# The last pair's products of h ordered by bank, one q load behind the late chunks, the rest of the values added a step later

## The chip, the cores and the metric

One Trainium2 chip, one of its cores. The metric is the device time of one execution in microseconds (us).

## The reference

Attention with pooled keys and values, and a gated layer behind it:

```python
k_p = k.reshape(B, H, Sp, 8, D).mean(axis=3)      # B=8, H=8, S=576, D=64, Sp=72
v_p = v.reshape(B, H, Sp, 8, D).mean(axis=3)
scores = scale * np.matmul(q, k_p.transpose(0, 1, 3, 2))
attn = softmax(scores)                             # with 1e-09 in the divisor
x = (attn @ v_p).transpose(0, 2, 1, 3).reshape(4608, 512)
h = x @ w_in                                       # 512 x 2048
g = h * np.clip(h + 3.0, 0.0, 6.0) / 6.0
out = g @ w_out                                    # 2048 x 512
```

All in float32; the kernel splits operands into a high and a low part and adds three matmuls for each product.

## The kernel before

The 4608 tokens are twelve blocks. The first four ("plain", `run`) go through the 16 slices f of the hidden size one by one: a product of h on PE (L847, into bank h0 or h1 by turns), relu on ACT (L855), the gate on DVE (L859), the high part on ACT (L863), the low part on DVE (L867), and two slices later the product with w_out (L878).

The last eight blocks go in four pairs, the super blocks n = 0 to 3 (`super_block`). Two slices of the hidden size, two halves of the input and the two blocks are each taken as a 2 x 2 matrix of blocks, and its product is made with seven products instead of eight. For each pair i of slices there are seven kinds o of products of h (L1140). Kinds 1, 6, 7 and 4 go into the pair's bank X, 5 and 3 into Y, 2 into Z. What comes behind a product: after 1, 5 and 6 ACT copies the bank (`keep`, L1113); after 2, 3 and 7 DVE adds bank and copy (`plus`, L1104) and the gate follows, relu on ACT (L1096) and the gate itself on DVE (L1098); after 4 the gate comes at once. A product into a bank whose reader is still due waits for it. The order of the products is the list `N1`, made from the table `PERIOD`, whose entries are a kind and by how many pairs it lags. Then comes the second half of the super block, the products with w_out (L1194 in n = 0, L1267 in the others, where g is split by L1119 on ACT and L1121 on DVE).

The weights of the seven products are made by `sums_of` during plain blocks 2 and 3 (DVE, tile wq), stored to DRAM (L954) and loaded again in each super block as chunks of two products, in the order of `N1`, 512 KB each (`chunk`, L998; wd0 to wd27 are the chunks in DRAM). There are seven places for chunks: four, wsFalse, are there from the middle of block 3, three, wsTrue ("late"), come free at its end. The hook `more` runs at the end of block 3: it takes the two first loads of the next pair's attention ahead, the q load and a load of the rest of the values (tile vr), and then loads the three late chunks.

Between the products stand the steps of the attention of later blocks: loads (q L241, k L249, v L285 and its rest vr L289), sums of eight values (`prep_v`, L384), the rest's high and low parts vrem (L410 on ACT, L411 on DVE), scores on PE (L464, kbd times qt), their maximum on DVE (mx, L468), exponentials on ACT (L473), sum and inverse on DVE (L490, L491), the division on POOL (L502), transposes (L573, L575), splits (alo L586, arem L597 and L599) and the product with the values (L647). `side_steps` gives the order of the loads (`load_v`) and of the additions (`prep_v`) of the values.

The code gives each step a place between products; the scheduler that builds the program then orders each engine's instructions by its own model of when each can run. An engine runs its queue strictly in order, SP's queue of DMAs too, and a DMA also waits until the eighth before it has landed.

Of the kernel before, what the change touches and what calls it, by code (L numbers as in the profile page):

```python
# [22 lines left out]
PLAIN = 4  # L23
# [12 lines left out]


PERIOD = ((1, 0), (2, 0), (7, 1), (5, 0), (6, 0), (4, 1), (3, 0))
RAW = {1: (0, 0), 2: (0, 1), 4: (1, 1)}
CHUNK, NSTREAM, NFIRST, NC, NREL = 2, 7, 4, 3, 2  # L40

# [57 lines left out]
def attention_moe_kernel(  # L99
# [20 lines left out]
    NB, _, NPAIR, S = q.shape  # L120
# [126 lines left out]
    def load_k(b, p):  # L247
        kraw[b, p] = ring("kst")
        nc.sync.dma_start(kraw[b, p], k[b, p])  # L249
        after_mark()  # L250
# [3 lines left out]
    def prep_k(b, p):  # L254

        two = b == 0
        if not two:
            ks = pool.tile([P, 1, SP], F32, name="ksum", bufs=1)
        elif p % 2 == 0:
            ks = ksum[p // 2] = piece(0, 2 * SP).rearrange("p (i s) -> p i s", i=2)  # L260
        else:
            ks = ksum[p // 2]
        i = p % 2 if two else 0
        nc.vector.tensor_reduce(
            out=ks[:, i], in_=kraw.pop((b, p)).rearrange("p (s o) -> p s o", o=POOL), axis=AX.X, op=ALU.add
        )
        after_mark()
        if i == two:

            scale = 1.0 / (POOL * D**0.5)  # L270
            for h in range(2):
                rows = slice(h * D, (h + 1) * D)
                nc.scalar.mul(kbds[b % 2][rows, p - i : p + 1, h * SP : (h + 1) * SP], ks[rows], scale)
# [3 lines left out]
    def load_v(b, p):  # L277

        own = late and b > 2 and p == NPAIR + 1
        t = vraw[b, p] = late[0].tile([P, POOL * D], F32, name="vr") if own else ring("vst")  # L280
        half = slice(p % 2 * (POOL // 2) * D, (p % 2 + 1) * (POOL // 2) * D)
        to = t[:, : POOL * D].rearrange("p (c n) -> p c n", c=2)
        p -= p % 2
        if p < NPAIR:
            nc.sync.dma_start(to, v[b, p : p + 2, :, half].rearrange("c r n -> r c n"))  # L285
            after_mark()
            return
        for c in range(3):
            nc.sync.dma_start(to[c * REM : (c + 1) * REM], vr[b, :, :, half].rearrange("g r n -> r g n"))  # L289
            after_mark()  # L290
# [366 lines left out]
    def side_steps(b):  # L657

        ks = [lambda p=p: load_k(b, p) for p in range(NPAIR)]
        ks += [lambda p=p: prep_k(b, p) for p in range(NPAIR)]  # L660
        if b > 2:
            order = ("load", 5), ("load", 4), ("load", 0), ("load", 1), ("prep", 4), ("load", 2), ("load", 3)
            order += ("prep", 0), None, ("prep", 2)
            do = {"load": load_v, "prep": prep_v}
            return ks, [(lambda x=x: do[x[0]](b, x[1])) if x else no_slot for x in order]
        vs = []
        n = NPAIR + NG
        for p in range(n):
            vs.append(lambda p=p: load_v(b, p))
            if p > 2 and p % 2:  # L670
                vs.append(lambda p=p: prep_v(b, p - 3))
        vs.append(lambda: prep_v(b, n - 2))
        return ks, vs
# [225 lines left out]
    class Paced:  # L899


        def __init__(self, steps, n, more=()):
            self.steps, self.n, self.at, self.done = steps, n, 0, 0
            self.more = list(more)
# [18 lines left out]


    NPR = NF // 2
    N1 = [(i, o) for t in range(NPR + 1) for o, d in PERIOD for i in [t - d] if 0 <= i < NPR]
    supers = range(PLAIN, len(BLOCKS), 2)
    w_dram = [tc.dram_tile([P, CHUNK, 2, 2 * P], F32, name=f"wd{n}") for n in range(len(N1) // CHUNK)]
    w2_dram = [tc.dram_tile([P, 4, 2, 2, DM // 2], F32, name=f"w2d{m}") for m in range(NF // 4)]
    w2t_dram = [tc.dram_tile([P, len(PLACED), 2, 2, DM // 2], F32, name=f"w2t{m}") for m in range(NF // 4)]  # L930

    def dram_of(i, o):
        n = N1.index((i, o))
        return w_dram[n // CHUNK][:, n % CHUNK]

    def pair_of(i):
        return [w_of[2 * i + r, 0].bitcast(F32).rearrange("p m (q c) -> p m q c", q=2) for r in range(2)]
# [18 lines left out]
    def store(to, src):  # L956
        nc.sync.dma_start(to, src)

    def plain_of(i, n):
        if n < 2:  # L960
            for o, (r, q) in list(RAW.items())[2 * n : 2 * n + 2]:
                store(dram_of(i, o), pair_of(i)[r][:, :, q])
# [116 lines left out]
    def super_block(n, j, first_att, second_att):  # L1079
# [4 lines left out]
        r_of, c_of = [], []  # L1084
        paced = Paced(first_att, len(N1) - 2)

# [40 lines left out]

        for m, (i, o) in enumerate(N1):
            if o == 1:
# [287 lines left out]
    later_steps = {}  # L1417
# [83 lines left out]
    def more():  # L1501

        early_x.pop().release()
        more_late.append(tc.alloc_tile_pool(name="late2", bufs=1, side="left", reuse_waits="tile"))
        n_lead = 2
        for pre, *_ in later_steps[PLAIN + 2]:
            while pre and n_lead:
                x = pre.pop(0)
                assert not isinstance(x, tuple) or x[0] == "load"
                (x[1] if isinstance(x, tuple) else x)()  # L1510
                n_lead -= 1
        chunk(0, NSTREAM - 1)

    make = [lambda i=i, h=h: sums_of(i, h) for i in range(NPR) for h in range(2)]
# [71 lines left out]
```

## Time and profile before

| what | value |
|---|---|
| runs | 891.61, 891.85, 892.01 us |
| median | 891.85 us |
| profiled execution, its own time | 891.74 us |
| span of the profile | 890.0 us |
| granted TensorE clock | 0.998 |
| DMA | 200.00 MB, mean 225 GB/s |

PE is the matmul, PEld the load of its weights, which runs ahead of the matmul; a wait stands in brackets behind the row that waited, with what it waited for. The stages lie so: plain blocks 2 and 3 from 217 to 348 us, the h stages of the super blocks at 348 to 426, 496 to 568, 632 to 702 and 767 to 826, and the products with w_out behind each.

### The profile page before, as it was taken

The numbers are of one execution on the slowest core, as the hardware profiler recorded it, in microseconds if no ns is written. First come the engines' busy times: TensorE is split into PE (matmuls) and PEld (weight loads), VectorE is DVE, ScalarE is ACT, GpSimd is POOL, SyncE is SP. The second block draws the span as 40 slices with busy tenths as digits, with TensorE's granted clock in tenths as the row PEclk, the third lists the DMA queues.
The fourth block names the chain that finished last, engine by engine and source line by source line (L and its number), as shares of the span: only waits on it lengthen the run. The fifth ranks groups of instructions, "written<-read, shape, count | busy, mean of one in ns | idle before, by whom it ended". The sixth has DMA issues, their size and how long they took to land.

```text
span 890.0 us, 15637 instructions
## 1 busy us (share of the span) xinstructions
PE 869.6 (98%) x5360; PEld 811.6 (91%) x5360; DVE 667.0 (75%) x1340; ACT 553.0 (62%) x1515; POOL 82.3 (9%) x168
## 2 busy tenths in 40 slices
PE   7899999999999999999999999999999999999998
PEld 7788888988989889999888999899999999999998
DVE  5999864567776785788889588997688877466664
ACT  5998666655666565778444677665576846355442
POOL 4100002110111100102000111100110200000000
PEclk9999999999999999999999999999999999999999
DMA  9980205996435253997596978887986777877884
GB/s 285 393 303 1 72 24 180 356 331 175 120 83 152 56 163 89 360 310 247 191 296 212 359 240 277 270 268 229 300 291 215 238 232 239 277 256 231 273 264 134
DMA packets 124654, 200.00 MB, mean 225 GB/s; under 512 B 13216, under 2 KB 81056, under 8 KB 124576
## 3 DMA queue, kind: packets, MB, share of 16 engines
q1 hardware_dynamic: 124432, 199.00, 68.6%
q8 instruction: 43, 0.70, 0.3%
q14 instruction: 35, 0.29, 0.1%
q10 hardware_dynamic: 144, 0.00, 0.0%
HBM read 158.08 MB, written 40.89 MB: 224 GB/s over the span
## 4 chain that ended last, share of the span: by engine, by line
PE 77%; DVE 9%; DMA 7%; ACT 4%; SPq 2%; issue 1%; DVEq 0%; ACTq 0%
PE psx L1140 23%; PE psx L1267 20%; PE pso L878 10%; PE psh L847 9%; PE psx L1194 8%; PE psa L647 3%; PE psa L464 3%; DMA wd<-wq 2%; DMA stage<-q_l 2%; ACT e L473 2%; SPq L954 1%; DVE wq L950 1%; PE psa L573 1%; DVE wq L945 1%; DMA qt<-q_l 1%
## 5 line engine op out<-in xcount | busy, mean ns | idle before, releaser
L1140 PE MATMUL psx<-x,wsFalse 128*128 128x384 f32 x768 | 150.5, 339 | 3.2 <-DVE g L1104 1.4
L847 PE MATMUL psh<-xhi,w 128*128 128x384 f32 (+2 forms) x520 | 146.2, 340 | 0.1
L1140 PEld LDWEIGHTS psx<-x,wsFalse 128*128 128x128 f32 x768 | 132.8, 188 | 5.0 <-DVE g L1104 1.8
L1119 ACT CAST part<-g 128x768 fp32r<-128x768 f32 x100 | 83.5, 837 | 79.6 <-PE psx L1267 59.5
L1121 DVE TENSOR_TENSOR part<-g,part 128x768 fp32r<-128x768 f32 x100 | 95.3, 954 | 39.5 <-ACT part L1119 39.2
L878 PE MATMUL pso<-w,ghi 128*128 128x512 f32 x384 | 120.7, 399 | 0.4 <-ACT o L883 0.4
L1140 PE MATMUL psx<-x,wsTrue 128*128 128x384 f32 x576 | 116.0, 340 | 0.1
L1267 PE MATMUL psx<-wsFalse,part 128*128 128x256 f32 x864 | 108.4, 282 | 0.4 <-ACT kept L1242 0.4
L1267 PEld LDWEIGHTS psx<-wsFalse,part 128*128 128x128 f32 x864 | 105.1, 188 | 1.0 <-ACT kept L1242 1.0
L1140 PEld LDWEIGHTS psx<-x,wsTrue 128*128 128x128 f32 x576 | 99.6, 188 | 1.1 <-DMA wsTrue<-wd 0.5
L847 PEld LDWEIGHTS psh<-xhi,w 128*128 128x128 f32 x520 | 93.3, 188 | 7.5 <-DVE g L859 0.4
L473 ACT ACTIVATE e<-psa,mx 128x72 f32<-128x72 f32 x256 | 79.0, 326 | 31.7 <-DVE mx L468 29.3
L502 POOL TENSOR_TENSOR a<-e,sm 128x256 f32<-128x256 f32 x60 | 40.3, 673 | 510.4 <-DVE sm L491 432.4
L847 PE MATMUL psh<-xlo,w 128*128 128x384 f32 (+2 forms) x260 | 87.1, 336 | 0.0
L1267 PE MATMUL psx<-wsTrue,part 128*128 128x256 f32 x648 | 80.6, 281 | 0.0
L878 PEld LDWEIGHTS pso<-w,ghi 128*128 128x128 f32 x384 | 68.9, 188 | 11.1 <-ACT o L883 0.8
L1267 PEld LDWEIGHTS psx<-wsTrue,part 128*128 128x128 f32 x648 | 78.6, 188 | 0.0
L1096 ACT ACTIVATE r<-g,small 128x384 f32<-128x384 f32 x96 | 58.6, 623 | 30.0 <-DVE g L1104 29.5
L878 PE MATMUL pso<-w,glo 128*128 128x512 f32 x192 | 74.6, 399 | 0.0
L1104 DVE TENSOR_TENSOR g<-psx,c 128x384 f32<-128x384 f32 x96 | 52.0, 553 | 27.4 <-PE psx L1140 20.7
L1098 DVE SCALAR_TENSOR_TENSOR g<-r,g 128x384 f32<-128x384 f32 x96 | 55.3, 587 | 12.1 <-ACT r L1096 11.5
L1113 ACT COPY c<-psx 128x384 f32<-128x384 f32 x96 | 44.9, 486 | 25.2 <-PE psx L1140 25.1
(140 smaller groups left out, 1476.1 us busy)
## 6 DMA issues: line engine op xcount, KB each, us to landing
wsFalse<-wd SPq DMA_DIRECT2D x64, 512.0 KB, 4.8
wsTrue<-wd SPq DMA_DIRECT2D x48, 512.0 KB, 4.8
wsFalse<-w2d SPq DMA_DIRECT2D x31, 512.0 KB, 5.3
wsFalse<-w2t SPq DMA_DIRECT2D x27, 512.0 KB, 4.8
wsTrue<-w2d SPq DMA_DIRECT2D x21, 512.0 KB, 5.0
wsTrue<-w2t SPq DMA_DIRECT2D x21, 512.0 KB, 4.8
raw<-w_in_l SPq DMA_DIRECT2D x16, 512.0 KB, 8.6
raw<-w_out_l SPq DMA_DIRECT2D x16, 512.0 KB, 9.2
```

What stands on the lines that cost most here:

```text
L473: nc.scalar.activation(self.e[:, h], self.ps[:, h], AF.Exp, bias=self.mx[:, h : h + 1], accum_out=self.sm[:, h : h + 1])
L847: nc.tensor.matmul(self.ps, l[f][:, c, :], r[:, c, :], start=c == 0 and i == 0, stop=c == NCC - 1 and i == 2)
L878: nc.tensor.matmul(pos, l, r, start=f == 0 and i == 0, stop=f == NF - 1 and i == 2)
L1096: nc.scalar.activation(r, src, AF.Relu, bias=half_low, scale=GSCALE / (6.0 * WSCALE))
L1098: nc.vector.scalar_tensor_tensor(out=g_of[i][:, k], in0=r, scalar=GSCALE, in1=src, op0=ALU.min, op1=ALU.mult)
L1104: nc.vector.tensor_tensor(out=g_of[i][:, k], in0=ps, in1=kept, op=ALU.add)
L1113: nc.scalar.copy(c, ps)
L1119: nc.scalar.copy(t[:, 0], src)
L1121: nc.vector.tensor_tensor(out=t[:, 1], in0=src, in1=t[:, 0].bitcast(F32), op=ALU.subtract)
L1140: nc.tensor.matmul(ps, w[:, l, c * P : (c + 1) * P], t[:, r, c], start=o in (1, 2, 5) and c == 0 and k == 0, stop=c == 1 and k == 2, skip_ ...
L1194: nc.tensor.matmul(to, l, w[:, qs, r], start=f == 0 and k == 0, stop=end and k == 2)
L1267: nc.tensor.matmul(to, t[:, l, k, i * P : (i + 1) * P], w[:, k, r], start=begin and k == 0 and y == 0 and i % 2 == 0, stop=m == NM - 1 and ...
```

## The change

```diff
 PERIOD = ((1, 0), (2, 0), (7, 1), (5, 0), (6, 0), (4, 1), (3, 0))
+LAST = ((1, 0), (7, 1), (2, 0), (6, 0), (5, 0), (4, 1), (7, 0), (3, 0), (4, 0))
...
         if b > 2:
-            order = ("load", 5), ("load", 4), ("load", 0), ("load", 1), ("prep", 4), ("load", 2), ("load", 3)
+            order = ("load", 5), ("load", 4), ("load", 0), ("load", 1), ("load", 2), ("prep", 4), ("load", 3)
...
-    N1 = [(i, o) for t in range(NPR + 1) for o, d in PERIOD for i in [t - d] if 0 <= i < NPR]
+    N1 = [(i, o) for t in range(NPR - 1) for o, d in PERIOD for i in [t - d] if 0 <= i < NPR]
+    N1 += [(NPR - 1 - d, o) for o, d in LAST]
...
-        n_lead = 2
-        for pre, *_ in later_steps[PLAIN + 2]:
-            while pre and n_lead:
-                x = pre.pop(0)
-                assert not isinstance(x, tuple) or x[0] == "load"
-                (x[1] if isinstance(x, tuple) else x)()
-                n_lead -= 1
+        loads = [(pre, x) for pre, *_ in later_steps[PLAIN + 2] for x in pre]
+        pre, x = loads[1]
+        pre.remove(x)
+        x()
         chunk(0, NSTREAM - 1)
```

There are three parts. The last nine products of `N1` come in another order, which also changes what chunks 24 to 27 hold. Of the two loads taken ahead in `more` only the second, vr, still is; the q load stays at its own place, behind the late chunks. And the addition of the rest of the values ("prep", 4) comes one load later. Behind the edits the lines of the changed kernel stand one or two further down (L464 is L465, L1140 is L1142, L998 is L1000).

PE, the end of plain block 3, before; pso is the product with w_out, psa of kbd and qt a group of scores, psh the next product of h:

```order
L878 MATMUL pso<-w_1006,ghi 128x512 x6
L464 MATMUL psa<-kbd_83,qt 128x144 x2
L878 MATMUL pso<-w_1006,glo 128x512 x3
L847 MATMUL psh<-xhi,w_1150 128x384
L847 MATMUL psh<-xlo,w_1150 128x384
```

The same place after:

```order
L879 MATMUL pso<-w_1006,ghi 128x512 x6
L879 MATMUL pso<-w_1006,glo 128x512 x3
L848 MATMUL psh<-xhi,w_1150 128x384
L848 MATMUL psh<-xlo,w_1150 128x384
L848 MATMUL psh<-xhi,w_1150 128x384 x2
```

The group of scores has left this place. It and the group that stood between the first products of super block 0 now stand there together, behind the products of the late chunks.

SP's DMAs around the start of super block 0, before; wq are the stores of the last weights, out is block 3's output, wsTrue and wsFalse are the places of the chunks wd:

```order
L954 DMA wd25_117<-wq_3910 128x2x128 x2
L884 DMA out<-o_3993 128x512
L884 DMA out<-o_3999 128x512
L884 DMA out<-o_4005 128x512
L998 DMA wsTrue_3968<-wd4_96 128x1024
L998 DMA wsTrue_3970<-wd5_97 128x1024
L998 DMA wsTrue_3972<-wd6_98 128x1024
L289 DMA vst_4042<-vr_l 32x2x256 x3
L241 DMA qt_4079<-q_l 128x4x128
L285 DMA vst_4081<-v_l 128x2x256
L998 DMA wsFalse_4108<-wd7_99 128x1024
```

And after:

```order
L956 DMA wd25_117<-wq_3910 128x2x128 x2
L885 DMA out<-o_3997 128x512
L885 DMA out<-o_4003 128x512
L1000 DMA wsFalse_4108<-wd7_99 128x1024
L1000 DMA wsTrue_3966<-wd4_96 128x1024
L1000 DMA wsTrue_3968<-wd5_97 128x1024
L1000 DMA wsTrue_3970<-wd6_98 128x1024
L242 DMA qt_4015<-q_l 128x4x128
L290 DMA vst_4042<-vr_l 32x2x256 x3
L242 DMA qt_4079<-q_l 128x4x128
L286 DMA vst_4081<-v_l 128x2x256
```

Chunk 7, which takes over the place of chunk 0, was the fourth chunk issued and is now the first, ahead of the three late chunks 4 to 6; the q load now stands behind them. On DVE, meanwhile, the addition of vr to vst came behind four additions and two gates of h, and comes behind five of each and a split now.

DVE, the end of the h stage of n = 1, before; g_6267 holds g of the last two pairs, psx,c an addition behind product 3 or 7, r,psx the gate behind product 4:

```order
L411 SCALAR_TENSOR_TENSOR vrem<-vst,small,vrem 32x2x64 x3
L1098 SCALAR_TENSOR_TENSOR g_6267<-r,g_6267 128x384 x2
L384 TENSOR_TENSOR vst<-vst 128x512
L468 TENSOR_REDUCE mx<-psa 128x4
L1104 TENSOR_TENSOR g_6267<-psx,c 128x384
L586 TENSOR_TENSOR alo<-psa,ahi 128x2x128
L1098 SCALAR_TENSOR_TENSOR g_6267<-r,psx 128x384
L586 TENSOR_TENSOR alo<-psa,ahi 128x2x128
L384 TENSOR_TENSOR vst<-vst 128x2x128
L1104 TENSOR_TENSOR g_6267<-psx,c 128x384
```

And after:

```order
L492 RECIPROCAL sm<-sm 128x4
L1100 SCALAR_TENSOR_TENSOR g_6267<-r,g_6267 128x384 x2
L385 TENSOR_TENSOR vst<-vst 128x512
L469 TENSOR_REDUCE mx<-psa 128x4
L1100 SCALAR_TENSOR_TENSOR g_6267<-r,psx 128x384
L385 TENSOR_TENSOR vst<-vst 128x2x128
L1106 TENSOR_TENSOR g_6267<-psx,c 128x384
L587 TENSOR_TENSOR alo<-psa,ahi 128x2x128
L385 TENSOR_TENSOR vst<-vst 128x2x64
L1106 TENSOR_TENSOR g_6267<-psx,c 128x384
```

The vrem pieces have gone further ahead, and the gate of the pair before and one piece of the sums of values now stand ahead of the addition that the last product waits for. PE's products at this place, and at the end of n = 3, stand in the same order in both kernels.

## The prediction

> **What bounds the kernel now.** First the head of the page, which gives the span and the engines' shares.
>
> ```profile
> span 890.0 us, 15637 instructions
> PE 869.6 (98%) x5360; PEld 811.6 (91%) x5360; DVE 667.0 (75%) x1340; ACT 553.0 (62%) x1515; POOL 82.3 (9%) x168
> ```
>
> PE is busy for 98% of the span, so the change, which takes no matmul away, can only win or lose PE's idle time. The profiled run took 891.74 us, 1.74 more than its span; the runs' median is 891.85, 0.1 above it. I add to 890.0 and then put the 1.74 back. A measurement of this kernel can tell about 0.2% from no change, 1.8 us.
>
> Next the view by windows, at the end of plain block 3, in the first h stage and in the second h stage.
>
> ```profile
> core 0: us, PE busy (x) PEld busy (x) DVE busy (x) ACT busy (x) POOL busy (x), PEclk, DMA share, GB/s
> 320.00:334.00 14.00, 12.80 (x68) 11.34 (x68) 13.90 (x23) 7.98 (x14) 0.00 (x0) 1.00 0.70 221
> 360.00:374.00 14.00, 13.14 (x75) 11.97 (x75) 10.64 (x27) 12.00 (x42) 1.73 (x4) 1.00 1.06 367
> 495.60:568.00 72.40, 70.67 (x429) 69.80 (x428) 57.69 (x131) 55.53 (x192) 12.17 (x25) 1.00 0.84 281
> 632.00:702.00 70.00, 70.00 (x438) 69.66 (x437) 56.73 (x131) 51.24 (x175) 9.76 (x18) 1.00 0.78 255
> ```
>
> The reader is to see three places where PE isn't full. In 320 to 334 DVE is: 13.90 of 14.00. In 360 to 374 the DMA engines are: share 1.06 at 367 GB/s. The third h stage (632 to 702) leaves PE no idle at all, so nothing is won there. The list of PE's waits names what the change can reach:
>
> ```profile
> PEld psx L1140 <- DVE g L1104: 1.9, 2, 1.8
> PEld psa L464 <- DMA qt<-q_l: 1.6, 1, 1.6
> PEld psx L1140 <- DVE vrem L411: 1.0, 1, 1.0
> PEld psx L1140 <- ACT c L1113: 0.9, 1, 0.9
> PEld psx L1140 <- DMA wsTrue<-wd: 0.5, 2, 0.3
> PEld psx L1140 <- ACT vrem L410: 0.4, 1, 0.4
> ```
>
> These six are 6.3 us; more than that the change cannot win here. It can also make new waits.
>
> **A. The q load moved back, end of block 3.** The timeline of PE's weight loads and of DVE:
>
> ```profile
> 305.01 0.20 PEld L573 LDWEIGHTS psa<-ident,a 128*128 128x128 f32 x2 [1.09 <-POOL a L502]
> 331.90 0.54 DVE L859 SCALAR_TENSOR_TENSOR g<-g,psh 128x384 f32<-128x384 f32 x1
> 332.96 0.54 PEld L464 LDWEIGHTS psa<-kbd,qt 128*128 128x128 f32 x4 [1.64 <-DMA qt<-q_l]
> 333.44 0.55 PEld L878 LDWEIGHTS pso<-w,glo 128*128 128x128 f32 x3
> 334.03 0.19 PEld L847 LDWEIGHTS psh<-xhi,w 128*128 128x128 f32 x1
> ```
>
> In the changed order the group of scores at 332.96 is gone from here, with its wait of 1.64 and its own 0.54; the 0.54 comes back inside the h stage, at no gain. Not all of the 1.64 is won. The next product of h (334.03) writes the bank that the gate at 331.90 reads, two products earlier, and that gate ends at 331.90 + 0.54 = 332.44, on an engine that is full. Without the scores PE would be there at 334.03 - 1.64 - 0.54 = 331.85 and wait until about 332.5. So the start moves from 334.03 to 332.5: 1.53, of which 0.54 is moved work. **A = -1.0.** The wait of 1.09 at 305.01 may go too, since DVE's order there changes, but PE then only meets the same gate earlier. Ends: -1.64 (the gate comes sooner) and -0.5 (DVE comes 0.5 later).
>
> **E. A chunk ahead of the late chunks, start of the h stage.** SP's queue and PE's products:
>
> ```profile
> 354.03 1.42 SPq L884 DMA_DIRECT2D out<-o  x3
> 355.54 1.54 SPq L998 DMA_DIRECT2D wsTrue<-wd  x3
> 360.34 0.41 SPq L998 DMA_DIRECT2D wsFalse<-wd  x1
> DMA to landing us min/median/max: 4.5/5.7/7.2
> 353.12 4.13 PEld L1140 LDWEIGHTS psx<-x,wsFalse 128*128 128x128 f32 x24
> 357.24 0.61 PEld L464 LDWEIGHTS psa<-kbd,qt 128*128 128x128 f32 x4
> 360.12 1.01 PEld L1140 LDWEIGHTS psx<-x,wsTrue 128*128 128x128 f32 x6 [0.26 <-DMA wsTrue<-wd]
> 363.81 1.69 PEld L1140 LDWEIGHTS psx<-x,wsTrue 128*128 128x128 f32 x10 [0.25 <-DMA wsTrue<-wd]
> ```
>
> The landing row is that of the three late chunks alone. Issued at 355.54, the first lands after 4.5 and PE waits 0.26 for it; the second takes 5.7, the third 7.2. In the changed order SP issues chunk 7, which goes into the place of chunk 0, ahead of these three. Chunk 0's second product is the second of the 24 loads from 353.12 (each product is six), so its place is free at about 353.12 + 2 x 1.03 = 355.2 plus the end of its matmul, when SP arrives at 355.5: no wait for the place. But chunk 4 is now second in the row, which is the 5.7 of that row: issued at about 356.0, landed at 361.7. PE, without the scores at 357.24 (0.54, moved), wants it at 360.12 - 0.26 - 0.54 = 359.32. New wait 2.4; the two old ones (0.26 and 0.25) go with it, as the later chunks have the same time again. **E = +1.9.** Ends: +0.7, if chunk 4 still lands 4.5 after its issue (360.5, a wait of 1.2), and +3.4, if it takes the third's 7.2 (363.2, a wait of 3.9).
>
> On the order: these three land one behind another. The Trainium skill, "DMA: Bandwidth & Descriptors", section "Queues, rings and completion order", says that each DMA engine consumes descriptors in ring order, which speaks against the changed order; the trace agrees with its 4.5, 5.7, 7.2. By it E stays +1.9. The same section says that a later write may finish before an earlier one, which alone would give rival 1; no row here shows that.
>
> **B. The rest of the values added later.** DVE and PE right behind:
>
> ```profile
> 364.64 0.69 DVE L384 TENSOR_TENSOR vst<-vst,vr 96x512 f32<-96x512 f32 x1 [2.43 <-DMA vst<-vr_l]
> 369.14 0.99 PEld L1140 LDWEIGHTS psx<-x,wsFalse 128*128 128x128 f32 x6 [0.44 <-ACT vrem L410]
> 371.14 1.01 PEld L1140 LDWEIGHTS psx<-x,wsFalse 128*128 128x128 f32 x6 [1.00 <-DVE vrem L411]
> ```
>
> DVE stands 2.43 for the rest's transfer with all gates queued behind it, and PE pays 0.44 + 1.00 later. In the changed order the addition stands behind three more gates, one more addition of h and one split, and the 2 us that PE loses in E let DVE and ACT catch up. **B = -1.4.** Other end: 0 or a little above, if the transfer, now issued behind a chunk and a q load, is late again.
>
> **C. The end of the second h stage.** DVE is saturated there:
>
> ```profile
> 552.14 0.56 DVE L1098 SCALAR_TENSOR_TENSOR g<-r,g 128x384 f32<-128x384 f32 x1 [0.35 <-ACT r L1096]
> 562.69 1.26 DVE L411 SCALAR_TENSOR_TENSOR vrem<-vst,small,vrem 32x128 fp32r<-32x128 f32 x3
> 565.89 0.54 DVE L1104 TENSOR_TENSOR g<-psx,c 128x384 f32<-128x384 f32 x1
> 566.49 1.01 PEld L1140 LDWEIGHTS psx<-x,wsFalse 128*128 128x128 f32 x6 [1.76 <-DVE g L1104]
> 566.69 0.54 DVE L1098 SCALAR_TENSOR_TENSOR g<-r,psx 128x384 f32<-128x384 f32 x1
> 567.49 0.41 DVE L384 TENSOR_TENSOR vst<-vst 128x256 f32<-128x256 f32 x1
> ```
>
> PE's last product waits 1.76 for the addition at 565.89. The new order puts the vrem pieces earlier, but they are still ahead of that addition, and so are now two pieces that stood behind it, the gate of 566.69 (0.54) and the 0.41: about 0.9 more. Against it, DVE stood idle on ACT for 0.35 at 552.14, and less a little before, which pieces that come earlier now fill. I take off 0.6 for both. **C = +0.3**; ends -1.3 (the vrem no longer in the way) and +0.9.
>
> **LAST.** By the order, the last products of the second and of the fourth h stage stand on PE as before: the scheduler had already spaced them. So I cost that part at nothing; what it does is move which chunk a product's weights lie in. The rest of the reordering (waits of 0.66 and 0.83 at the end of the first h stage, a little more of the attention on DVE in the third) I cost at 0, with -1.5 and +1.5 as ends, which are the two waits below going, or coming again elsewhere:
>
> ```profile
> 418.22 0.54 PEld L464 LDWEIGHTS psa<-kbd,qt 128*128 128x128 f32 x4 [0.66 <-DVE arem L599]
> 421.92 0.19 PEld L647 LDWEIGHTS psa<-ahi,vhi 128*128 128x128 f32 x1 [0.83 <-ACT e L473]
> ```
>
> **Sum**: -1.0 + 1.9 - 1.4 + 0.3 + 0 = -0.2. Span 889.8, and with 1.74 **891.5 us**: what is won at two waits is paid at a new one.
>
> **The rivals.**
> 1. *The extra chunk doesn't hold the late ones* (E = +0.7): 891.5 - 1.2 = 890.3, on the border of what can be told. For it: the DMA engines are idle much of the time before 355, share 0.70 in 320 to 334. Against it: three chunks in a row landed later each.
> 2. *Slower: the row of transfers becomes the bound.* Chunk 7, the late three, two q loads and the rest all queue at SP in order, and from 360 the DMA share is 1.06. If chunk 4 takes the third's 7.2 (E = +3.4) and the rest's transfer is late again (B = 0): 891.5 + 1.5 + 1.4 = 894.4. It decides from where chunk 4 lands later than about 363.
> 3. *LAST does what it says.* If bank order is what the last products wait on, the 1.76 above and this 0.89 both vanish:
>
> ```profile
> 824.16 2.04 PEld L1140 LDWEIGHTS psx<-x,wsFalse 128*128 128x128 f32 x12 [0.89 <-ACT c L1113]
> ```
>
> That is 891.5 - 0.3 - 1.76 - 0.89 = 888.6. Against it: the order of those products on PE is the same. The Trainium skill, "PSUM — Partial Sum Buffer", section "PSUM bank collisions raise a hardware error", has one engine at a time on a bank, guarded by bank; by it, products on one bank spaced further apart would wait less. The trace agrees that a bank's reader ends these waits (1.76, 0.89), but here the spacing does not change.
>
> **How the numbers follow.** Forecast 0.55, rival 1 0.18, rival 2 0.15, rival 3 0.12. Below 890.1 (0.2% under 891.85) lie rival 3, a little under half of rival 1 (0.08) and 0.10 from the forecast's own spread (A and C at their low ends): 0.30. Above 893.6 lie rival 2 and 0.07 of the forecast: 0.22. Within: 0.48. Range: 888.8 leaves out half of rival 3, 894.2 half of rival 2 and a little of the tails: 888.8 to 894.2.
>
> **What would show it.** A: no wait for q near 333, a wait of the h product for the gate of about 0.6 in its place. E: PE idle about 2.4 at its first late chunk, near 359. B: no wait for vrem near 370, and DVE not idle before the addition of the rest. C: the wait before the last h product of the second stage still near 2. LAST: the 0.89 at 824 still there. The forecast is wrong by E first of all: a landing that differs by 2 us moves it across the border of 0.2%.

## The result, and the profile after

The changed kernel took 894.58 us (median of 9 runs, 891.25 to 898.58), the kernel before 891.28 in the same session (9 runs, 887.72 to 892.43). The comparison puts the ratio at **1.0053, 95% interval 1.0034 to 1.0072**: slower by some 4.7 us. (The ratio is not the quotient of the two medians, which lie 3.3 us apart.) The forecast was 891.5 and no change that can be told; the range ended at 894.2. The profiled execution of the changed kernel took 894.79 us, its span is 893.0, 3.0 more than before.

The head of its page, two rows of its view by windows (columns as in the one of before), and its list of PE's waits (what waited for what; us in sum, times, longest):

```profile
span 893.0 us, 15642 instructions
PE 869.4 (97%) x5360; PEld 811.5 (91%) x5360; DVE 664.6 (74%) x1340; ACT 552.7 (62%) x1515; POOL 84.6 (9%) x168
```

```profile
360.00:374.00 14.00, 14.00 (x87) 13.97 (x86) 11.77 (x29) 11.77 (x39) 1.98 (x4) 1.00 1.08 365
632.00:702.00 70.00, 69.53 (x439) 68.93 (x437) 55.34 (x131) 51.23 (x176) 11.84 (x21) 1.00 0.80 259
```

```profile
PEld psx L1142 <- DVE g L1106: 3.4, 3, 1.3
PEld psx L1142 <- ACT c L1115: 3.2, 4, 1.1
PEld psa L465 <- issue: 2.8, 1, 2.8
```

PE does the same work (869.4 busy, 869.6 before) in 3.0 us more. Where the transfers had been at 1.06 and PE idle, from 360 to 374, PE is now full; but the third h stage (632 to 702), which had been full, has 0.47 idle. The waits that the change aimed at, for q and for vrem, have left the list. New ones stand at its top: the additions of h on DVE, the copies c on ACT, and one of 2.8.

Where the 3.0 us lie is read from the timeline of the weight loads: the place of the same instruction in both traces, from which the lengths follow. The marks are the last product with w_out in block 1 that waited (before 203.39, after 201.69), the first product of h of the four super blocks (for n = 2 and 3 its second group of weight loads, since five loads of h stand already among the products with w_out; before 348.63, 496.08, 632.61, 766.98; after 344.21, 496.62, 633.82, 768.86) and the ends of the spans (890.0, 893.0).

| stretch | before | after | difference |
|---|---|---|---|
| up to block 1 | 203.39 | 201.69 | -1.70 |
| plain blocks 2 and 3 | 145.24 | 142.52 | -2.72 |
| super block n = 0 | 147.45 | 152.41 | +4.96 |
| n = 1 | 136.53 | 137.20 | +0.67 |
| n = 2 | 134.37 | 135.04 | +0.67 |
| n = 3 | 123.02 | 124.14 | +1.12 |

The plain blocks win what was promised and more (0.54 of the 2.72 is the group of scores that moved on), and super block 0 gives it back with 2.24 on top, of which 1.7 is a halved clock, shown below. The h stage of super block 0 first, at its start. PE and its weight loads, then DVE, then ACT, all of the changed kernel:

```profile
349.90 3.10 PEld L1142 LDWEIGHTS psx<-x,wsFalse 128*128 128x128 f32 x18 [1.18 <-ACT o L884]
354.08 3.07 PEld L1142 LDWEIGHTS psx<-x,wsFalse 128*128 128x128 f32 x18 [1.09 <-DVE g L1106]
358.45 6.19 PEld L1142 LDWEIGHTS psx<-x,wsTrue 128*128 128x128 f32 x36 [1.29 <-DVE g L1106]
358.48 6.48 PE L1142 MATMUL psx<-x,wsTrue 128*128 128x384 f32 x36 [1.00 <-DMA wsTrue<-wd]
```

```profile
345.74 0.76 DVE L947 TENSOR_TENSOR wq<-w 128x256 f32<-128x256 f32 x2 [2.13 <-DMA wd<-wq]
348.90 0.69 DVE L954 TENSOR_TENSOR wq<-wq 128x512 fp32r<-128x512 f32 x1 [0.73 <-ACT wq L953]
353.47 0.56 DVE L1106 TENSOR_TENSOR g<-psx,c 128x384 f32<-128x384 f32 x1 [3.88 <-DMA wd<-wq]
...
357.52 0.56 DVE L1106 TENSOR_TENSOR g<-psx,c 128x384 f32<-128x384 f32 x1
```

```profile
348.25 0.62 ACT L953 CAST wq<-wq 128x512 fp32r<-128x512 f32 x1 [3.58 <-DVE wq L952]
348.77 1.57 ACT L884 ACTIVATE o<-pso 128x512 f32<-128x512 f32 x3
```

And DVE of the kernel before at the same two instructions:

```profile
347.89 0.75 DVE L945 TENSOR_TENSOR wq<-w 128x256 f32<-128x256 f32 x2
355.59 0.56 DVE L1104 TENSOR_TENSOR g<-psx,c 128x384 f32<-128x384 f32 x1 [3.65 <-PE psx L1140]
```

PE comes to the stage 4.42 us earlier than before (344.21 for 348.63), but the last sum of weights begins only 2.15 earlier (345.74 for 347.89), since it now stands 2.13 for the stores of the sum ahead of it, which leave the one tile wq. ACT's cast of that sum waits 3.58 for it, with the three copies of block 3's output (o) queued behind, and PE waits 1.18 for the second of those, which ends at 349.85. DVE's first addition of h used to wait for PE; now it waits for the last store, and PE waits 1.09 for the addition. The third wait is for the first late chunk, which lands at about 358.3; the addition named in the weight loads' row had ended at 357.52 + 0.56 = 358.08.

Then the end of that h stage, on SP, DVE and PE:

```profile
412.52 0.56 SPq L286 DMA_DIRECT2D vst<-v_l  x1
```

```profile
417.59 0.69 DVE L385 TENSOR_TENSOR vst<-vst 128x512 f32<-128x512 f32 x1 [2.64 <-DMA vst<-v_l]
...
418.67 0.68 DVE L385 TENSOR_TENSOR vst<-vst 128x512 f32<-128x512 f32 x1
419.38 0.29 DVE L600 TENSOR_TENSOR arem<-psa,arem 32x128 fp32r<-32x128 f32 x1
```

```profile
419.82 1.29 PE L465 MATMUL psa<-kbd,qt 128*128 128x144 f32 x4 [2.55 <-DVE arem L600]
```

DVE stands 2.64 for a load of values that SP issued only at 412.52. Behind that addition are queued a gate, a second addition and the split arem, for which the next scores on PE wait: 2.55 on the matmul, 2.84 on the weight loads. In the kernel before such a split stood ahead of the first such addition, and PE waited 0.66 and 0.83 here:

```profile
417.88 0.29 DVE L599 TENSOR_TENSOR arem<-psa,arem 32x128 fp32r<-32x128 f32 x1
...
420.84 0.68 DVE L384 TENSOR_TENSOR vst<-vst 128x512 f32<-128x512 f32 x1
```

And right behind, the view by windows of 1 us; the third column from the end is the granted TensorE clock:

```profile
419.00:420.00 1.00, 0.18 (x1) 0.21 (x2) 0.94 (x3) 0.00 (x0) 0.00 (x0) 0.91 0.73 242
420.00:421.00 1.00, 1.00 (x5) 1.00 (x6) 0.97 (x4) 0.29 (x2) 0.00 (x0) 0.50 0.51 193
421.00:422.00 1.00, 1.00 (x5) 1.00 (x4) 1.00 (x5) 1.00 (x9) 0.00 (x0) 0.50 0.10 41
422.00:423.00 1.00, 1.00 (x5) 0.90 (x4) 0.84 (x3) 0.95 (x5) 0.00 (x0) 0.50 0.00 0
423.00:424.00 1.00, 1.00 (x8) 1.00 (x7) 0.93 (x4) 0.79 (x4) 0.00 (x0) 0.88 0.00 0
```

After the idle 2.55 us the clock is halved for about 3.4 us, which costs 0.09 + 3 x 0.50 + 0.12 = 1.7 us. The kernel before has such a stretch too in its profile, elsewhere, from 13 to 17 us, right behind this wait of PE:

```profile
12.89 5.35 PE L347 MATMUL psa<-stage,ident 128*128 128x128 f32 x31 [1.98 <-DMA stage<-v_l]
...
14.00:15.00 1.00, 1.00 (x7) 1.00 (x6) 1.00 (x7) 0.10 (x1) 0.56 (x2) 0.50 1.01 383
```

The profile of the change has none there, which may be the -1.70 of the table's first row; but in the profiles of the experiments that have none there either, this row lies anywhere from -0.2 to -1.8.

The second and the third super block lose 0.67 each. PE's weight loads and ACT at the end of both h stages:

```profile
559.02 1.00 PEld L1142 LDWEIGHTS psx<-x,wsTrue 128*128 128x128 f32 x6 [0.49 <-ACT c L1115]
561.12 0.99 PEld L1142 LDWEIGHTS psx<-x,wsFalse 128*128 128x128 f32 x6 [1.10 <-ACT c L1115]
567.66 1.01 PEld L1142 LDWEIGHTS psx<-x,wsFalse 128*128 128x128 f32 x6 [1.00 <-DVE g L1106]
701.95 0.99 PEld L1142 LDWEIGHTS psx<-x,wsFalse 128*128 128x128 f32 x6 [0.70 <-ACT c L1115]
```

```profile
560.57 0.49 ACT L1115 COPY c<-psx 128x384 f32<-128x384 f32 x1
...
701.42 0.48 ACT L1115 COPY c<-psx 128x384 f32<-128x384 f32 x1
```

The copies at 560.57 and 701.42 have no wait of their own: ACT is busy right up to them, at 701 with a group of exponentials and two casts of the attention. Before, ACT stood idle ahead of the copy in the third stage, waiting for PE:

```profile
699.21 0.48 ACT L1113 COPY c<-psx 128x384 f32<-128x384 f32 x1 [1.07 <-PE psx L1140]
```

The +1.12 of n = 3 is one chunk that landed late, a wait of 1.39 at 804.14; among the kernels below such a wait comes and goes.

### The profile page after: what moved, and what is told of

Same layout as the page of the kernel before. It is cut to its first block, busy times and chain, and to the rows that moved or that the text cites. A ratio compares the mean times of both kernels' runs of the same rounds, so it can differ in the third digit from the quotient of the medians.

```text
span 893.0 us, 15642 instructions
## 1 busy us (share of the span) xinstructions
PE 869.4 (97%) x5360; PEld 811.5 (91%) x5360; DVE 664.6 (74%) x1340; ACT 552.7 (62%) x1515; POOL 84.6 (9%) x168
## 4 chain that ended last, share of the span: by engine, by line
PE 70%; DVE 11%; DMA 8%; ACT 5%; SPq 2%; issue 2%; POOL 0%; DVEq 0%; ACTq 0%; POOLq 0%
PE psx L1142 21%; PE psx L1269 20%; PE psh L848 8%; PE psx L1196 8%; PE pso L879 7%; DMA wd<-wq 4%; PE psa L648 3%; PE psa L465 3%; ACT e L474 2%; SPq L956 2%; DVE wq L952 2%; DVE wq L947 1%; DMA wsTrue<-wd 1%; DMA raw<-w_in_l 1%; DVE x L1046 1%
## 5 line engine op out<-in xcount | busy, mean ns | idle before, releaser
L1142 PE MATMUL psx<-x,wsFalse 128*128 128x384 f32 x768 | 151.8, 340 | 4.4 <-ACT c L1115 1.8
L1142 PEld LDWEIGHTS psx<-x,wsFalse 128*128 128x128 f32 x768 | 132.6, 188 | 6.7 <-ACT c L1115 2.7
L1142 PE MATMUL psx<-x,wsTrue 128*128 128x384 f32 x576 | 116.1, 342 | 2.5 <-DMA wsTrue<-wd 2.1
L1142 PEld LDWEIGHTS psx<-x,wsTrue 128*128 128x128 f32 x576 | 100.6, 189 | 3.6 <-issue 1.4
```

What stands on the lines that cost most here:

```text
L1142: nc.tensor.matmul(ps, w[:, l, c * P : (c + 1) * P], t[:, r, c], start=o in (1, 2, 5) and c == 0 and k == 0, stop=c == 1 and k == 2, skip_ ...
```

## The experiments

The theories in the expectations: B, that at these places DVE and ACT have no room for work that comes another way, so that removing one late transfer only brings out the next wait; C, that the row of sums through the one tile wq holds the start of the h stage; D, that the landing of the late chunks holds it. Theories 1 to 3 and A are said in the expectations themselves. The runs of the kernel before at the same time, on the same chip, gave medians of 888.1 to 889.1 us in these sessions; ratios are to them.

**The three parts, one by one, and two of them.** First the order of the last products alone.

```diff
-    N1 = [(i, o) for t in range(NPR + 1) for o, d in PERIOD for i in [t - d] if 0 <= i < NPR]
+    N1 = [(i, o) for t in range(NPR - 1) for o, d in PERIOD for i in [t - d] if 0 <= i < NPR]
+    N1 += [(NPR - 1 - d, o) for o, d in LAST]
```

> Only the order of the last products (LAST); the two loads taken ahead and the order of the values as before. Theory 1 (the loss comes from the moved q load and the later addition together, at the end of the first h stage): no change, within 1.5 us of before, and the 0.89 before the last products of the fourth h stage is still there. Theory 2 (the later addition alone holds a place of the ring too long): the same. Theory 3 (the moved q load alone, by the order of the chunks): the same. Rival of all three: LAST itself costs, then 3 us or more slower.

Measured: 1.0016 (1.0001 to 1.0032).

The q load alone:

```diff
-        n_lead = 2
...
+        loads = [(pre, x) for pre, *_ in later_steps[PLAIN + 2] for x in pre]
+        pre, x = loads[1]
```

> Only the q load behind the late chunks. Theory 1: faster by 1 to 3 us, since the wait of 1.64 for q at the end of plain block 3 goes and the end of the first h stage keeps its waits of under 1 us. Theory 2: the same. Theory 3: slower by 3 us or more.

Measured: 1.0023 (1.0005 to 1.0040).

The order of the values alone:

```diff
-            order = ("load", 5), ("load", 4), ("load", 0), ("load", 1), ("prep", 4), ("load", 2), ("load", 3)
+            order = ("load", 5), ("load", 4), ("load", 0), ("load", 1), ("load", 2), ("prep", 4), ("load", 3)
```

> Only the addition of the rest of the values one load later. Theory 1: within 2 us of before, no wait over 2 us at the end of the first h stage. Theory 2: slower by 3 us or more, with DVE waiting over 2 us for a load of the values there. Theory 3: within 2 us of before.

Measured: 1.0018 (1.0006 to 1.0030).

The q load and the values together, with the old order of products (both diffs above):

> The q load and the later addition, the last products in the old order. Theory 1: as slow as the whole change, 3 to 5 us over before, with DVE waiting some 2.6 us for a load of the values at the end of the first h stage, PE idle for over 2 us behind it and its granted clock at 0.50 for some 3.4 us after. Theory 2: as slow as the addition alone. Theory 3: as slow as the q load alone.

Measured: 1.0041 (1.0024 to 1.0059). Theory 1 has the sum right (3.6 us), but not its parts: by it the q load alone would have been faster, and it was some 2 us slower. Theory 3 asked for 3 us or more there, theory 2 for 3 us or more of the values alone, which cost 1.6. No part is the gain or the loss by itself. The stretches, against the profile of before as in the table above, with the loss to the halved clock in n = 0 taken out of the third column (its own column). The last row is the kernel before profiled once more, with 1.7 of halved clock taken out of its n = 1; it shows how far a stretch moves with no change at all:

| kernel | blocks 2, 3 | n = 0 without clock | clock in n = 0 | n = 1 | n = 2 |
|---|---|---|---|---|---|
| order of products | -1.6 | -0.1 | 0 | -0.1 | +0.2 |
| q load | -2.0 | +1.9 | 1.7 | -0.1 | 0.0 |
| values | -2.2 | +2.1 | 0 | +0.6 | +0.7 |
| q load and values | -3.6 | +3.6 | 0 | +0.7 | +0.7 |
| the whole change | -2.7 | +3.3 | 1.7 | +0.7 | +0.7 |
| the kernel before again | +0.4 | -0.6 | 0 | -0.2 | 0.0 |

The q load and the values each win about 2 us in the plain blocks and each lose about 2 in super block 0: the two stretches together are -0.1, -0.1 and 0.0 with one or both, and +0.5 with the whole change. What is left is the 0.65 in n = 1 and the 0.7 in n = 2, which come with the values, and the clock. Of the 2.0 us that the q load costs by its ratio, the mean granted clock of its runs (0.9987 for 0.9991) explains 0.4; where the rest lies these profiles don't show. The gain in the plain blocks is uncertain by itself: the order of products doesn't touch them, and yet shows -1.6 there, and the kernel before once more +0.4. With the order of products the wait for q was shorter in its execution, and the 1.09 at 305.01 was not there:

```profile
331.19 0.54 PEld L465 LDWEIGHTS psa<-kbd,qt 128*128 128x128 f32 x4 [1.02 <-DMA qt<-q_l]
```

The waits at the start of the h stage are not the same with both parts. With the values alone PE waits 1.11 for the copies of o and 0.82 for an addition of h, as in the change. With the q load alone these are absent: PE waits 1.02 for the first late chunk, and 1.36 at 367.13 for something that the profile doesn't name.

**The late load at the end of n = 0.** The changed kernel with the old order of the values for batch 5, whose values are added there.

```diff
             order = ("load", 5), ("load", 4), ("load", 0), ("load", 1), ("prep", 4), ("load", 2), ("load", 3)
+            if b != 5:
+                order = ("load", 5), ("load", 4), ("load", 0), ("load", 1), ("load", 2), ("prep", 4), ("load", 3)
```

> The whole change, but the pair of q, k and v whose sums stand at the end of the first h stage (batch 5) keeps the old order of loads and additions. Theory A (the wait of 2.84 at the end of the first h stage, and the half clock that follows it in many executions, is the largest single piece of the loss): 2 to 3 us faster than the whole change, so 0.1 to 0.3% over before, PE's waits there back under 1.5 us, the 0.6 in the second and the 0.7 in the third h stage still lost. Theory B (the scheduler deals the order anew, and a wait of that size comes up in another place): as slow as the whole change, with another wait of over 2 us.

Measured: 1.0047 (1.0031 to 1.0063). Its weight loads at the end of the stage:

```profile
414.81 1.00 PEld L1144 LDWEIGHTS psx<-x,wsTrue 128*128 128x128 f32 x6 [1.58 <-DVE g L1108]
416.69 0.20 PEld L574 LDWEIGHTS psa<-ident,a 128*128 128x128 f32 x2 [0.88 <-POOL ar L509]
418.30 0.99 PEld L1144 LDWEIGHTS psx<-x,wsTrue 128*128 128x128 f32 x6 [1.30 <-ACT c L1117]
420.23 0.99 PEld L1144 LDWEIGHTS psx<-x,wsTrue 128*128 128x128 f32 x6 [0.94 <-DVE g L1108]
```

The 2.84 is gone, and four waits of 4.7 in sum stand in its place; the clock stays up in this profile, and n = 0 is 3.3 longer than before, as with the whole change. So A, which asked for 2 to 3 us less, fails. The late load was what ended last there; with it gone, other waits took its place.

**The row of sums.** A store of a sum goes out by ACT's queue for two of the four products, in the changed kernel, in the one with the q load alone, and in the kernel before.

```diff
-            nc.sync.dma_start(dram_of(i, o)[:, :, half], t[:, :, at])
+            (nc.scalar if at % 2 else nc.sync).dma_start(dram_of(i, o)[:, :, half], t[:, :, at])
```

> The whole change, and two of the four stores of each sum of weights go out from ACT's queue instead of SP's. Theory C (what is won at the end of plain block 3 is given back at the start of the first h stage, because the chain of the last sums of weights, DVE, stores, landing, next sum in the same tile, ends when it did): a sum's period falls from 8.9 to about 8 us, the first addition of the first h stage comes 1 to 2 us sooner and PE's three waits there (1.18, 1.09, 1.29) shrink to under 2 us together; the time falls by 1 to 2 us against the whole change. Theory D (the start of the first h stage is bound by the landing of the late chunks): no change there.

> The q load behind the late chunks alone, with the stores on two queues. Theory C: 1 to 2 us faster than the q load alone, so 0 to 0.1% off before. Theory D: as the q load alone, 0.2% over before.

> The kernel before with the stores on two queues. Theory C: within 1 us of before, since there the q wait and not the chain of sums is what PE waits for at the end of plain block 3 and DVE waits for PE at the start of the first h stage. Theory D: the same. If it is faster by over 1 us, the chain bounded the kernel before as well.

Measured: 1.0061 (1.0039 to 1.0083), 1.0057 (1.0038 to 1.0076) and 1.0035 (1.0020 to 1.0050). One sum did follow another sooner: in the first of these after 7.70 us and the next after 8.82 (8.94 and 9.11 in the kernel with the order of products alone), though the last then waited 3.02 for the stores to land. But the last sum began no earlier, at 346.84 for the change's 345.74, since the sums ahead of it stood 2.70 later (330.32 for 327.62). The kernel before lost by the edit alone, with new waits of 1.58 and 1.09 at the start of the h stage that look like those of the change (1.18 and 1.09): its blocks 2 and 3 were 4.6 shorter and its n = 0 was 6.0 longer. So this says little on C, as the end of the row of sums didn't come sooner; it shows once more that what PE wins ahead of this stage it loses in it.

**The last store taken away.** The last sum is worked out but not stored; its four stores take raw halves of w_in.

```diff
+        last = (i, h) == (NPR - 1, 1)
         for o, at in {7: 0, 3: 1, 5: 2, 6: 3}.items():
-            nc.sync.dma_start(dram_of(i, o)[:, :, half], t[:, :, at])
+            src = pair_of(i)[at // 2][:, :, at % 2, half] if last else t[:, :, at]
+            nc.sync.dma_start(dram_of(i, o)[:, :, half], src)
```

> The changed kernel, but the four stores of the very last sum take raw halves of w_in instead of the tile wq, so that this sum's result is never stored and the products 3, 5, 6 and 7 of the last pair take wrong weights in one half; the sum itself is still worked out. DVE's first addition of h (L1106) then no longer has to wait until those stores have landed. The scheduler also shifts other instructions. Theory C (the room of wq, freed by the last stores, holds the first addition and with it PE): the bracket 3.88 for wd<-wq at the first addition goes, the three waits of PE at the start of the first h stage (1.18, 1.09, 1.29) come down to about 1 us in sum, and the span from the start of the stage to the first product with w_out is about 2 us shorter than in the changed kernel; ratio about 1.002 to 1.003. Theory B (DVE and ACT simply have too much work left at that point): those waits stay near 3 us; ratio about 1.005.

> The kernel before with the same edit (the last sum's four stores take raw halves of w_in). In the kernel before, the first addition waits for PE, not for a store, so both theories expect the start of the first h stage to be as it was, apart from what the scheduler shifts: ratio 0.999 to 1.001. The difference of the two kernels with this edit is the loss of the change without the last stores: about 2 us by theory C, about 4 us by theory B.

Measured: 1.0050 (1.0034 to 1.0066) for the change with it, 1.0005 (0.9992 to 1.0019) for the kernel before with it. The weight loads of the changed kernel with this edit, at the start and at the end of the stage, and DVE's first addition:

```profile
350.73 3.07 PEld L1144 LDWEIGHTS psx<-x,wsFalse 128*128 128x128 f32 x18 [1.39 <-ACT o L884]
354.59 1.01 PEld L1144 LDWEIGHTS psx<-x,wsTrue 128*128 128x128 f32 x6 [0.80 <-ACT r L1100]
...
420.85 1.01 PEld L1144 LDWEIGHTS psx<-x,wsTrue 128*128 128x128 f32 x6 [2.75 <-DVE g L1108]
```

```profile
353.16 0.53 DVE L1108 TENSOR_TENSOR g<-psx,c 128x384 f32<-128x384 f32 x1
```

The wait for the store is gone, and the addition still comes at 353.16 (353.47 with it): DVE, one row ahead, had to wait for exponentials on ACT instead. The start's waits fall from 3.56 to 2.19, neither to C's 1 nor staying at B's 3, but the stage gives it back at its end, and the difference of the two kernels is 4.1 us by their medians (893.34 less 889.28), little less than the 4.7 without the edit. So the store, and with it C, is not the cause of the loss. Nor is D: SP issued the late chunks at 350.67 here and at 353.44 in the change, PE's first product on one came at 354.62 for 358.48, and n = 0 was still 150.5 long, for 150.7 in the change with the clock's 1.7 taken out. That a wait taken away brings out the next one, as B has it, is what was seen here and with batch 5. That DVE and ACT have too much to do is not shown: over the 78 us from the first product of h on, DVE was busy for 58.1 us in the change and 61.5 before, ACT for 55.9 and 60.5. It fits better that they do their work in an order in which PE waits; that is argued, since no run here changed their work alone.

**The values of the last batches.** The changed kernel with the old order of the values for batches 6 and 7, and the kernel before with the new order for these two alone:

```diff
+            if b < 6:
+                order = ("load", 5), ("load", 4), ("load", 0), ("load", 1), ("load", 2), ("prep", 4), ("load", 3)
```

> The changed kernel with the old order of the values for batches 6 and 7, whose additions stand in the second and third h stage. If the new order of just these batches makes the waits there (0.49 and 1.10 at 559 to 561, 0.70 at 702), the second h stage is 0.6 us and the third about 0.7 us shorter again: ratio about 1.004, 1.3 us under the changed kernel. If the losses come from what the earlier batches leave behind (buffers, banks, the state of the queues), these stages stay as in the changed kernel: ratio about 1.005.

```diff
+            if b > 5:
+                order = ("load", 5), ("load", 4), ("load", 0), ("load", 1), ("load", 2), ("prep", 4), ("load", 3)
```

> The kernel before with the new order of the values for batches 6 and 7 alone. Up to the end of the first super block nothing that runs on an engine should differ but by the scheduler. If these batches make the loss of the second and third h stage, the second is 0.6 us longer and the third 0.7 us longer: ratio about 1.0015. If it comes from the earlier batches: ratio 1.000.

Measured: 1.0064 (1.0043 to 1.0084) and 1.0013 (1.0001 to 1.0025). The weight loads of the kernel before with these two batches changed:

```profile
556.34 0.99 PEld L1142 LDWEIGHTS psx<-x,wsTrue 128*128 128x128 f32 x6 [0.48 <-ACT c L1115]
558.43 1.00 PEld L1142 LDWEIGHTS psx<-x,wsFalse 128*128 128x128 f32 x6 [1.10 <-ACT c L1115]
564.99 1.01 PEld L1142 LDWEIGHTS psx<-x,wsFalse 128*128 128x128 f32 x6 [1.00 <-DVE g L1106]
...
699.26 0.99 PEld L1142 LDWEIGHTS psx<-x,wsFalse 128*128 128x128 f32 x6 [0.69 <-ACT c L1115]
```

These are the four waits of the whole change, to 0.01, with n = 1 and n = 2 longer by 0.66 and 0.67, and the other stretches behind block 1 within 0.4 of before. In the other kernel they are gone (n = 1 -0.1, n = 2 +0.2, and the old 1.76 is back). This part is settled: 1.3 us of the loss come from the values of batches 6 and 7. That the other kernel is no faster in time has its reason in n = 0, where the load of values came later still, PE stood 4.06 for the split behind it, and a halved clock followed:

```profile
419.55 0.69 DVE L385 TENSOR_TENSOR vst<-vst 128x512 f32<-128x512 f32 x1 [4.11 <-DMA vst<-v_l]
```

**The level, and the order of products once more.** The kernel before against itself, then the order of products with the values, and with the q load (the diffs above).

> The kernel before, unchanged, put in the place of a changed kernel. If the comparison itself is level, the ratio is 1.000 and its interval holds 1. If a kernel in this place comes out about 0.1 per cent slower whatever it is, the 1.0016 of the new order of products by itself is mostly that, and that part of the change costs nothing; the other ratios are then too high by the same.

> The new order of the last products and the new order of the values, with the q load at its old place. If the new order of products costs 0.15 per cent of its own, it adds to the values' 1.0018: about 1.0034. If it costs nothing, this kernel is as the values alone: about 1.0018. The second and third h stage are 0.6 and 0.7 us longer in both.

> The new order of the last products and the q load at its own place, with the old order of the values. If the new order of products costs 0.15 per cent of its own, it adds to the 1.0023 of the q load: about 1.0038. If it costs nothing: about 1.0023. The second and third h stage are as in the kernel before.

Measured: 1.0002 (0.9989 to 1.0014), 1.0015 (1.0001 to 1.0030) and 1.0057 (1.0037 to 1.0077). The comparison is level. With the values the order of products costs nothing (1.0015 for 1.0018); with the q load it seems to cost 0.3%, though the two intervals overlap. In the profile of that kernel n = 0 without the clock is 2.0 longer, as with the q load alone (1.9); but PE's wait at 420 was 2.33, and the clock stayed halved behind it for twice as long, 3.4 us lost; it fell once more in n = 1. The mean granted clock of its runs is 0.9970, of those with the q load alone 0.9987: 1.5 us of 890, about half of the difference. What the order of products costs by itself stays open between nothing and 0.15%. None of these kernels was faster than the one before.

## Why the prediction was wrong

The forecast was a span of 889.8, and it became 893.0. By its own steps:

- **The step that failed** is "the rest of the reordering", costed at 0 with ends of -1.5 and +1.5. It took in the two waits of 0.66 and 0.83 at the end of the first h stage, which became one of 2.84: +1.2 with the 0.15 behind them. It took in the attention in the third stage, where the view by windows had shown PE without idle time and so "nothing is won"; that nothing could be lost did not follow: +0.67. And no term of the sum held waits at the start of the h stage for ACT and DVE (1.18 and 1.09). These are no accidents of one execution: the third stage's comes with the values of batches 6 and 7 alone, and two such waits at the start (1.11 and 0.82) with the values alone.
- **A** was right as an event and as far as it was followed. The wait for q is gone, and the gate takes its place, with 1.02 on the weight load and 0.58 on the matmul, for the forecast 0.6:

```profile
329.75 0.19 PEld L848 LDWEIGHTS psh<-xhi,w 128*128 128x128 f32 x1 [1.02 <-DVE g L860]
```

  The stretch won 2.72, where A with its moved work gave 1.53; the order of products, which doesn't touch this place, showed 1.6 as well. But "what is late next" was asked only up to the next gate. One stage further stand the last sums, their casts and stores and DVE's first addition, which came 2.15 earlier while PE came 4.42 earlier.
- **E** was right in place, and too large: chunk 7 does go ahead, and PE waits for the first late chunk at 358.48 (forecast near 359), but 1.00 on the matmul, 1.29 on the weight load, for 2.4. The term that was mis-sized is the landing. The three late chunks landed 4.9 to 6.6 after their issue, for 4.5 to 7.2 before, so that the chunk ahead cost the first of them 0.4 and not the 1.2 that was taken:

```profile
353.44 1.42 SPq L1000 DMA_DIRECT2D wsTrue<-wd  x3
DMA to landing us min/median/max: 4.9/5.7/6.6
```

  That is nearer to rival 1's case. The rule of ring order in the Trainium skill ("DMA: Bandwidth & Descriptors", "Queues, rings and completion order") was on the side of a wait; the three do land one behind another, at a third of the price. PE also came to the chunk sooner: 3.7 after its issue, for 4.3 before. Had it not lost 2.27 at the two waits ahead, it would have stood here for that much longer, with the chunk issued as it was.
- **B** was right: no wait for vrem is left, and DVE adds the rest of the values without idle time ahead of it:

```profile
363.49 0.68 DVE L385 TENSOR_TENSOR vst<-vst,vr 96x512 f32<-96x512 f32 x1
```

- **C** was mis-sized: +0.67 for +0.3. The last product waits 1.00 and not 2, but two new waits (0.49 and 1.10) stand ahead of it, behind ACT and not DVE, on which the working was made.
- **LAST** was right for its place: the 0.89 is still there, at 827.21. As a part by itself it measured 1.0016 at the edge of what can be told.
- **The clock** was in no step, though the profile of before held such a stretch: 1.7 us of n = 0 in this profile, as much as the profile of before lost near 13 us, so that it cancels between the two. Over the runs the mean granted clock is 0.9978, before 0.9991 to 0.9994: about 1.2 us of the 4.7.

With these, n = 0 adds up: waits at the start 3.56 for 1.95 (0.26, 0.25, 0.44, 1.00), +1.6; at the end 2.84 for 1.64, +1.2; the clock +1.7; and the group of scores that moved in, +0.5: 5.0, measured 4.96. All stages, the moved group and the clock left out: -2.2 in the plain blocks, +1.6 and +1.2 at the start and the end of n = 0, +0.7, +0.7 and +1.1 in the other three: 3.1, measured 3.0. The +1.1 of n = 3 was in no term either; in the experiments that stretch lies between 0.6 below before and 1.0 above. Rival 2 came out at 894.4, near the time measured, for a reason that did not hold: it needed chunk 4 later than 363, and the rest's transfer late.

What stays open is the cause in n = 0. The experiments show that it takes back what the plain blocks win, with the q load (+1.9) and the values (+2.1) apart, and that neither the last store, nor the landing of the late chunks, nor one late load is the cause by itself. Of the 4.7 us of the runs, 1.3 come from the values of batches 6 and 7, about 1.2 go with the clock, and some 2.2 are not placed.

## What to carry to other kernels

When an edit takes a wait away in one stage, follow the engine's gain past the next wait to the stage where the other engines' rows of work end; a gain that only lets one engine arrive early is not yet won. A stage in which the main engine has no idle time has nothing to win but still something to lose, so a reordering of side work there has a one-sided range, not zero. Test a part by the stretches of the trace as well as by its time: 0.66 us in one stage is plain there when the runs can hardly tell it. Profile the unchanged kernel twice to know what a stretch is good for: here its two profiles differed by 0.4 and 0.6 in the plain blocks and n = 0, and by 0.2 or less in the next two super blocks, with the clock taken out.

## What the runs showed of the hardware

The halved clock came behind shorter idle times of PE than expected, and not every time. One wait shows it best. At the end of the second h stage PE's matmuls wait 1.43 or 1.44 in nine of the profiles here. Behind it the clock fell in two of them, the kernel before once more and the order of products with the q load, and not in the other seven, that of the kernel before among them. The longest wait without a fall behind it is 3.11 (the q load and the values). PE's rows of the kernel before once more, and of that one:

```profile
565.64 1.77 PE L1140 MATMUL psx<-x,wsFalse 128*128 128x384 f32 x5 [1.44 <-DVE g L1104]
```

```profile
418.85 0.73 PE L464 MATMUL psa<-kbd,qt 128*128 128x144 f32 x4 [3.11 <-DVE arem L599]
```

The record of the clock in the traces says more. Every stretch at one clock but the last, which the end cuts off, is 3.413 us or a whole multiple of it. Laid on that grid, PE's matmuls were busy for at most 51% of the 3.413 us just ahead of each of the twelve falls inside these kernels. From where the record of the clock begins, every window at full clock with 42% or less was followed by a fall; of those from 44 to 51% some were and some were not. The wait of 3.11 lay across two windows, with 64 and 44% busy. By these figures it matters how much of one such window PE is idle, and so where a wait falls on the grid, and not the length of the wait alone.

Each such stretch lasted 3.4 us and cost about 1.7, in two cases twice that. The Trainium skill, "TensorE: Matmul & The Clock Gate", section "HAM oscillation — how this bites in real kernels", gives gaps of over about 3.4 us as the ones to avoid; here gaps well under that were enough, and the measurement decides. Its section "What's actually happening" says that the window in which the activity is judged runs freely, which agrees with a drop that comes in one execution and not in another. This also bears on the spread of the runs: the kernel before ran between 886 and 892 us in these sessions, with granted clocks from 0.995 to 1.0.
